# The last stage's second layer as seven block products

## The chip, the cores and the metric

The kernel runs on one core of a Trainium2 chip. The metric is device time in microseconds (us): the time from the start to the end of one execution. The core has five engines with a queue of instructions each, worked off in program order: TensorE (PE in the profile; its weight loads are PEld), VectorE (DVE), ScalarE (ACT), GpSimd (POOL) and SyncE (SP), which here issues the transfers. An engine waits for another only where an instruction needs what the other has yet to write, read or free.

## What is computed

Attention over a window of 64 keys, then a mixture of four experts, then one wide layer with a sloped activation:

```python
x = attention(q, k, v)                         # 1152 tokens x 512
for e in range(4):                             # experts: 512 -> 1024 -> 512
    out += p[:, e:e + 1] * (np.maximum(x @ w1[e], 0) @ w2[e])
x = out
h = x @ w_in                                   # 512 -> 2048
g = np.maximum(h, 0.0) + alpha * np.minimum(h, 0.0)
return g @ w_out                               # 2048 -> 512, alpha: one slope per column of h
```

Inputs are float32 (`w_in` and `w_out` float64, which the kernel converts itself).

## The kernel before, in words

**Precision.** Each float32 operand is kept as two parts that TensorE can multiply: a high part `h` (rounded) and a low part `l` (what rounding left). A product is three matmuls: low x high, high x low, high x high. Making the two parts of a tile is called a split: ACT copies the tile to `h`, and DVE or POOL subtracts `h` from the tile to get `l`.

**Stages.** After the attention, the hidden columns are worked off in 12 stages of 512: stages 0 to 7 are the experts, 8 to 11 the wide layer. `S1` is 8 and `NST` is 12, so the last stage is `s = 11`. The tokens are in two parts, `p = 0` with 512 and `p = 1` with 640. A stage runs through a hand-written list `order`: the first layer for part 0 (units `("A", s, 0, i)`, i from 0 to 6), the first layer for part 1 (`("A", s, 1, i)`), then the second layer for one tile of 128 tokens at a time (`("B", s, p, t)`, four tiles in part 0 and five in part 1).

**First layer.** It is already computed by seven block products instead of eight (`PRODUCTS`, function `product`). Unit i does the product i for both halves of the hidden columns (u = 0, 1), 6 matmuls each, with 256 columns (part 0) or 320 (part 1). The products accumulate in three PSUM banks per u, named X, Z and W; the sequence of banks over i is X, Z, X, W, X, Z, X. After i = 0, 1, 2 ACT copies the bank out (`keep`, L458: tiles s, z, u). After i = 3, 4, 5 DVE adds the bank to the copy (`total`, L462), and the result goes to `evict`; after i = 6 the bank X itself does. So each next use of a bank waits until the copy or the addition before it has read the bank.

**Activation in stages 8 to 11.** `evict` lets ACT make the negative part `r` (L498) and puts the rest in a list. `activate(keep, later)` takes it from there, a few at a time: DVE forms the activated value from `r`, the slope and the source (L541, `heads`), later ACT rounds it to `hh` (L545) and POOL subtracts to get `hl` (L546, `tails`). A part has eight such pieces.

**Second layer.** `l2_unit` makes one token tile by 12 matmuls of 128x512 (four blocks of hidden columns, three matmuls each; L565); DVE adds the bank to `acc` (L588), and in stage 11 SP writes the tile to the output (L590). The very last tile is cut into two halves of 256 columns.

**Order of the work around the matmuls.** Behind each unit's matmuls the program issues: what `settle` holds (the DVE half of earlier weight splits, L215), then the functions that `plan(unit, fn, ...)` hung on that unit, in the order of planning. In stage 11 these are four splits of the second layer's weights: `split_w2`, f = 0 and 1 on the units i = 0 and 1 of part 0, f = 2 and 3 on those of part 1. PSUM has eight banks, handed out in the order in which they were freed.

The functions, with the profile's line numbers:

Of the kernel before, what the change touches and what calls it, by code (L numbers as in the profile page):

```python
# [8 lines left out]
F32 = mybir.dt.float32  # L9
F32R = mybir.dt.float32r  # L10
BF16 = mybir.dt.bfloat16
U32 = mybir.dt.uint32
AF = mybir.ActivationFunctionType
# [13 lines left out]
def tile_kernel(ctx, tc, q, k, v, probs, w1, w2, w_in, w_out, alpha, out):  # L27
# [43 lines left out]
    def psum(name):  # L71
        return pp.tile([P, 512], F32, tag="ps", name=name)
# [419 lines left out]
    def evict(s, p, f, half, src, direct=False):  # L492
        c = slice(half * HALF[p], (half + 1) * HALF[p])
        hh, hl = [x[:, c] for x in h_tiles(s, p, f)]
        if s >= S1:
            col = (s - S1) * NF + f
            r = late["mid"].tile([P, HALF[1]], F32, tag="r", bufs=3, name=f"r{s}_{p}_{f}_{half}")[:, 0:HALF[p]]
            nc.scalar.activation(out=r, in_=src, func=AF.Relu, scale=-1.0)  # L498
            heads.append((hh, hl, r, alph[:, col:col + 1], src, r if direct else src))
            return  # L500
        nc.scalar.activation(out=hh, in_=src, func=AF.Relu)
        lows.append((hl, src, hh))
# [58 lines left out]
    def l2_products(s, p, t, cols, ps):  # L561
        n = 0
        for f in (1, 3, 0, 2) if s == S1 else range(NF):
            for a, b in ((0, 1), (0, 0), (1, 0)):
                nc.tensor.matmul(ps, lhsT=h_t[s, p, f][a][:, t * P:(t + 1) * P], rhs=w_t[2, s, f][b][:, cols],  # L565
                                 start=(n == 0), stop=(n == 3 * NF - 1))
                n += 1

    def l2_unit(s, p, t):

        cut = 2 if (s, p, t) == (NST - 1, 1, NTT[1] - 1) else 1
        w = DM // cut
        for x in range(cut):
            ps = psum(f"o{s}_{p}_{t}")[:, 0:w]
            cols = slice(x * w, (x + 1) * w)
            l2_products(s, p, t, cols, ps)
            l2_out(s, p, t, cols, ps)

    def l2_out(s, p, t, cols, ps):
        at = acc[p][:, t, cols]  # L580
# [20 lines left out]
    with tc.manual_schedule():  # L601
# [59 lines left out]
        def A(s, p):  # L661
            return [("A", s, p, i) for i in range(7)]

        def Bt(s, p):
            return [("B", s, p, t) for t in range(NTT[p])]
# [28 lines left out]
            order += A(s, 0) + A(s, 1) + Bt(s, 0) + Bt(s, 1)  # L694
        order += A(S1, 0) + [("B", S1, 0, t) for t in (2, 3, 0, 1)]
        order += A(S1, 1) + [("B", S1, 1, t) for t in (3, 4, 0, 1, 2)]
        for s in range(S1 + 1, NST):
            order += A(s, 0) + A(s, 1) + Bt(s, 0) + Bt(s, 1)
        at = {u: n for n, u in enumerate(order)}


# [5 lines left out]
        for s in range(1, NST):  # L707
            if s == 1:
                lc, b = [[(k, NCH - 1, t) for t in range(3)] for k in ("LC", "BC")]
                for u in range(2):  # L710
                    plan(lc[u], w_sums, (1, s), s, u, nc.gpsimd)
                for u, part, unit in ((0, A11, ("X1",)), (1, A11, b[0]), (0, SA1, b[0]), (1, SA1, b[1]),
                                      (0, A22, b[2]), (1, A22, b[2])):
                    plan(unit, w_split, (1, s), s, u, part)
            else:
                b = [("B", s - 1, x, t) for x in range(2) for t in range(NTT[x])]
                if s == S1 + 1:
                    b = [("B", S1, 1, t) for t in (3, 3, 4, 4, 0, 1)]
                late_sums = s > S1 + 1
                behind = 2 * (s > S1 + 1)  # L720
                plan(b[1] if behind else ("A", s - 1, 1, 0 if s > S1 else 2), w_sums, (1, s), s, 0, nc.gpsimd)
                for n, part in ((0, A11), (0, A22), (1 + behind, SA1)):
                    plan(b[n], w_split, (1, s), s, 0, part)
                plan(b[2 + behind], w_sums, (1, s), s, 1, nc.gpsimd)
                for n, part in ((2, A11), (3, A22), (4 + behind, SA1)):
                    plan(b[n], w_split, (1, s), s, 1, part)
            units = [(0, 0), (0, 1), (1, 0), (1, 1)]
            if s in (1, S1):
                units = [(int(s == 1), i) for i in (0, 0, 1, 1)]
            for f, (p, i) in enumerate(units):  # L730
                plan(("A", s, p, i), split_w2, (2, s), s, f)

        half = {p: [(0, HALF[p] // 2), (HALF[p] // 2, HALF[p] // 2)] for p in range(2)}
        first, second = half[0]
# [64 lines left out]
        for i, unit in enumerate(order):  # L799
# [9 lines left out]
            if op == "A":  # L809
                product(unit[1], unit[2], 0, unit[3])  # L810
                product(unit[1], unit[2], 1, unit[3])
                if unit[3] == 6:
                    low_parts(0)
                    activate(0, 0 if unit[1] == S1 else 4)
            elif op == "LC":
                l1_chunk(*unit[1:])
            elif op == "BC":
                l2_chunk(*unit[1:])
            elif op == "B":
                activate(0, max(0, len(tails) - 2) if unit[2] == 0 else 0)  # L820
                l2_unit(*unit[1:])
                if unit[1] == S1 - 1:
                    pend.append((i + 2, unit[2], unit[3]))
# [57 lines left out]
```

## Time and profile before

| | us |
|---|---|
| median of 3 runs | 615.28 (614.58 to 616.58) |
| profiled execution, whole | 615.4 |
| its span, first to last instruction | 613.2 |
| PE busy in the span | 604.5 (99%) |
| last stage, first layer, part 0 | 562.75 to 572.82 |
| last stage, first layer, part 1 | 572.82 to 585.14 |
| last stage, second layer | 585.14 to 609.97 |

Times in the profile count from the span's start. A matmul is pipelined: its row lasts longer than the distance to the next one's start, and it is this distance that sets the pace. In rows of instructions, "out<-in" are tiles by name, and the shape is partitions x elements.

### The profile page before, as it was taken

The numbers are of one execution on the slowest core, as the hardware profiler recorded it, in microseconds if no ns is written. First come the engines' busy times: TensorE is split into PE (matmuls) and PEld (weight loads), VectorE is DVE, ScalarE is ACT, GpSimd is POOL, SyncE is SP. The second block draws the span as 40 slices with busy tenths as digits, with TensorE's granted clock in tenths as the row PEclk, the third lists the DMA queues.
The fourth block names the chain that finished last, engine by engine and source line by source line (L and its number), as shares of the span: only waits on it lengthen the run. The fifth ranks groups of instructions, "written<-read, shape, count | busy, mean of one in ns | idle before, by whom it ended". The sixth has DMA issues, their size and how long they took to land.

```text
span 613.2 us, 10950 instructions
## 1 busy us (share of the span) xinstructions
PE 604.5 (99%) x4072; PEld 547.9 (89%) x4072; DVE 469.5 (77%) x946; ACT 318.0 (52%) x795; POOL 271.4 (44%) x278
## 2 busy tenths in 40 slices
PE   6999999999999999999999999999999999999997
PEld 5998999889889889989989989989898988988986
DVE  4887497799798798798698698667968989754642
ACT  5976356426427426426515525436777653642630
POOL 4756502075163254265152452522755585661440
PEclk9999999999999999999999999999999999999999
DMA  9951004234334325324234323012302402400012
GB/s 319 328 200 36 1 1 151 80 110 154 110 103 156 91 98 170 107 70 170 105 100 145 117 87 104 17 69 83 125 1 91 168 18 87 131 25 1 2 54 101
DMA packets 31365, 62.60 MB, mean 102 GB/s; under 512 B 2384, under 2 KB 11344, under 8 KB 30288
## 3 DMA queue, kind: packets, MB, share of 16 engines
q1 hardware_dynamic: 30880, 61.38, 29.7%
q8 instruction: 32, 0.52, 0.4%
q10 hardware_dynamic: 432, 0.52, 0.2%
q14 instruction: 21, 0.17, 0.1%
HBM read 51.14 MB, written 10.75 MB: 101 GB/s over the span
## 4 chain that ended last, share of the span: by engine, by line
PE 97%; DMA 1%; DVE 1%; ACT 0%; POOL 0%; ACTq 0%; issue 0%; POOLq 0%
PE o L565 44%; PE X L451 23%; PE Z L451 11%; PE W L451 6%; PE h L520 4%; PE oc L553 4%; PE pt L360 1%; PE pv L377 1%; PE s L322 1%; DMA kt<-in_k_dram 1%; PE x L598 1%; PE pt L307 0%; ACT p L344 0%; DVE ptr L364 0%; POOL p L353 0%; ACTq L125 0%
## 5 line engine op out<-in xcount | busy, mean ns | idle before, releaser
L565 PE MATMUL o<-w2l,hh 128*128 128x512 f32 (+1 forms) x400 | 155.5, 389 | 0.0
L565 PE MATMUL o<-w2h,hl 128*128 128x512 f32 (+1 forms) x400 | 155.3, 388 | 0.0
L565 PE MATMUL o<-w2h,hh 128*128 128x512 f32 (+1 forms) x400 | 154.9, 387 | 0.0
L294 POOL TENSOR_TENSOR ct<-ct 128x512 f32<-128x512 f32 x32 | 44.2, 1382 | 116.5 <-DVE ct L293 53.6
L565 PEld LDWEIGHTS o<-w2h,hl 128*128 128x128 f32 x400 | 75.1, 188 | 16.7 <-POOL hl L546 1.2
L565 PEld LDWEIGHTS o<-w2h,hh 128*128 128x128 f32 x400 | 75.1, 188 | 14.6
L565 PEld LDWEIGHTS o<-w2l,hh 128*128 128x128 f32 x400 | 75.1, 188 | 14.6
L584 DVE SCALAR_TENSOR_TENSOR acc<-o,pn,acc 128x512 f32<-128x512 f32 x63 | 47.1, 747 | 38.8 <-PE o L565 38.5
L190 POOL TENSOR_TENSOR sr<-ws 128x256 f32<-128x256 f32 x44 | 41.3, 938 | 73.7 <-DVE wfl L215 61.4
L215 DVE SCALAR_TENSOR_TENSOR w2l<-ws,w2h 128x512 fp32r<-128x512 f32 x48 | 44.1, 927 | 19.9 <-ACT w2h L222 19.8
L451 PE MATMUL X<-xth,wfl 128*128 128x256 f32 (+1 forms) x264 | 56.8, 296 | 0.0
L451 PE MATMUL X<-xth,wfh 128*128 128x256 f32 (+1 forms) x264 | 56.6, 295 | 0.0
L451 PE MATMUL X<-xtl,wfh 128*128 128x256 f32 (+1 forms) x264 | 56.6, 295 | 0.0
L222 ACT ACTIVATE wfh<-sr 128x1024 fp32r<-128x1024 f32 x22 | 23.2, 1059 | 53.4 <-POOL sr L190 53.4
L295 POOL TENSOR_TENSOR ct<-ct 128x512 f32<-128x512 f32 x32 | 47.2, 1476 | 2.5
L282 ACT ACTIVATE ct<-wd 128x512 f32<-128x512 f32 x32 | 21.4, 668 | 48.0 <-DVE ct L288 48.0
L588 DVE TENSOR_TENSOR acc<-o,acc 128x512 f32<-128x512 f32 (+1 forms) x28 | 18.8, 670 | 32.9 <-PE o L565 32.8
L451 PEld LDWEIGHTS X<-xth,wfh 128*128 128x128 f32 x264 | 42.6, 190 | 0.0
L451 PEld LDWEIGHTS X<-xtl,wfh 128*128 128x128 f32 x264 | 42.6, 190 | 0.0
L451 PEld LDWEIGHTS X<-xth,wfl 128*128 128x128 f32 x264 | 42.6, 190 | 0.0
L546 POOL TENSOR_TENSOR hl<-s,hh 128x256 fp32r<-128x256 f32 (+1 forms) x16 | 13.3, 851 | 61.3 <-ACT hh L545 61.3
L451 PE MATMUL Z<-xth,wfl 128*128 128x320 f32 (+1 forms) x176 | 37.9, 297 | 0.0
(156 smaller groups left out, 1408.5 us busy)
## 6 DMA issues: line engine op xcount, KB each, us to landing
ws<-in_moe_w_dram SPq DMA_DIRECT2D x16, 1024.0 KB, 6.1
wd<-in_moe_w_in_dram SPq DMA_DIRECT2D x16, 512.0 KB, 3.8
cv<-ct SPq DMA_DIRECT2D x32, 256.0 KB, 2.4
wd<-in_moe_w_out_dram SPq DMA_DIRECT2D x16, 512.0 KB, 3.6
ws<-cv SPq DMA_DIRECT2D x8, 1024.0 KB, 5.2
v<-in_v_dram SPq DMA_DIRECT2D x16, 256.0 KB, 5.8
out_dram<-acc SPq DMA_DIRECT2D x8, 256.0 KB, 2.0
q<-in_q_dram SPq DMA_DIRECT2D x4, 384.0 KB, 6.6
```

Source lines behind the costliest of these rows:

```text
L190: e.tensor_tensor(out=t4[:, o], in0=x, in1=y, op=op)
L215: nc.vector.scalar_tensor_tensor(out=lv, in0=src, scalar=1.0, in1=hv.bitcast(F32), op0=ALU.mult, op1=ALU.subtract)
L222: nc.scalar.activation(out=hv, in_=src, func=AF.Copy)
L282: nc.scalar.activation(out=a, in_=top.bitcast(F32), func=AF.Abs, scale=LIFT)
L294: nc.gpsimd.tensor_tensor(out=y, in0=y, in1=e, op=ALU.mult)
L295: nc.gpsimd.tensor_tensor(out=y, in0=r, in1=y, op=ALU.add)
L451: nc.tensor.matmul(ps, lhsT=w[:, d, :], rhs=x[:, d, :], start=(first and m == 0), stop=(m == 5), skip_group_check=True)
L520: nc.tensor.matmul(ps, lhsT=w[:, d * P:(d + 1) * P], rhs=x[:, d, :], start=(m == 0), stop=(m == 3 * KD - 1))
L553: nc.tensor.matmul(ps, lhsT=h_c[c, f][a][:, t * P:(t + 1) * P], rhs=w_t[2, 0, f][b], start=(n == 0), stop=(n == 3 * NF - 1))
L565: nc.tensor.matmul(ps, lhsT=h_t[s, p, f][a][:, t * P:(t + 1) * P], rhs=w_t[2, s, f][b][:, cols], start=(n == 0), stop=(n == 3 * NF - 1))
L584: nc.vector.scalar_tensor_tensor(out=at, in0=ps, scalar=sc, in1=at, op0=ALU.mult, op1=ALU.add)
L588: nc.vector.tensor_tensor(out=at, in0=ps, in1=at, op=ALU.add)
```

## The change

In stage 11 the second layer of eight of the nine token tiles is also computed by seven block products. The 512 hidden columns, the 512 output columns and 512 tokens of a part are each halved (blocks of 256); `block_product(p, n)` does product n of `BLOCKS` for the two tiles x = 0, 1 of 128 tokens, 6 matmuls of 128x256 each, into banks X, W and Z (two of each), and after every product and x DVE adds the bank to the part of `acc` that it belongs to. The bank goes on accumulating: the sequence is X, W, X, Z, X, Z, X. The units are `("M", p, n)`. The fifth tile of part 1 stays a unit `("B", 11, 1, 4)`, no longer cut in two and now between the two parts.

For these products sums of blocks are needed. `form_sums(key, half)` makes four for the weights (key `"t"`) and four for the activations of each part (keys 0 and 1), two DVE subtractions or additions of 128x512 at a time, out of SBUF tiles into SBUF tiles. `form_split(key, n, engine)` splits one: an ACT copy and a POOL subtraction of 128x512. So that the activated values are there unsplit, DVE's L541 now writes them to a tile of their own (`whole`). The `plan` calls hang this work on units of the first layer and of part 0's products. New `raw` tiles take two buffers in turn (`wd`), the rest lies in tiles that have served their use. In an `M` unit at most one of the `tails` that are left is done ahead of its matmuls.

```diff
@@ -496,7 +496,8 @@
             col = (s - S1) * NF + f
             r = late["mid"].tile([P, HALF[1]], F32, tag="r", bufs=3, name=f"r{s}_{p}_{f}_{half}")[:, 0:HALF[p]]
             nc.scalar.activation(out=r, in_=src, func=AF.Relu, scale=-1.0)
-            heads.append((hh, hl, r, alph[:, col:col + 1], src, r if direct else src))
+            g = whole(p)[:, f, c] if s == NST - 1 else r if direct else src
+            heads.append((hh, hl, r, alph[:, col:col + 1], src, g))
             return
         nc.scalar.activation(out=hh, in_=src, func=AF.Relu)
         lows.append((hl, src, hh))
@@ -567,14 +568,103 @@
                 n += 1
 
     def l2_unit(s, p, t):
-
-        cut = 2 if (s, p, t) == (NST - 1, 1, NTT[1] - 1) else 1
-        w = DM // cut
-        for x in range(cut):
-            ps = psum(f"o{s}_{p}_{t}")[:, 0:w]
-            cols = slice(x * w, (x + 1) * w)
-            l2_products(s, p, t, cols, ps)
-            l2_out(s, p, t, cols, ps)
+        ps = psum(f"o{s}_{p}_{t}")
+        l2_products(s, p, t, slice(0, DM), ps)
+        l2_out(s, p, t, slice(0, DM), ps)
+
+    HC = DM // 2
+    forms, banks = {}, {}
+
+    def whole(p):
+        if ("g", p) not in forms:
+            if p == 0:
+                forms["g", p] = sb.tile([P, NF, LEN[0]], F32, tag="ws", bufs=2, name="g0")
+            else:
+                forms["g", p] = moe.tile([P, NF, LEN[1]], F32, tag="xth0", name="g1")
+        return forms["g", p]
+
+    def form_tiles(key):
+        if key == "t":
+            t = sb.tile([P, 3584], F32R, tag="big", name="th")
+            u = late["wfp"].tile([P, 1024], F32R, tag="sr", bufs=1, name="tl3")
+            hi = [t[:, 2 * HC * n:2 * HC * (n + 1)] for n in range(4)]
+            lo = [t[:, 2 * HC * (4 + n):2 * HC * (5 + n)] for n in range(3)] + [u[:, 0:2 * HC]]
+        elif key == 0:
+            t, (u, w) = xt[0][1].rearrange("p a k t -> p (a k t)"), [x.rearrange("p k t -> p (k t)") for x in xa[0]]
+            hi = [t[:, 2 * HC * n:2 * HC * (n + 1)] for n in range(4)]
+            lo = [y[:, 2 * HC * n:2 * HC * (n + 1)] for y in (u, w) for n in range(2)]
+        else:
+            return [[x[:, n, :, 0:HC] for n in range(4)] for x in xt[1]]
+        return [[x.rearrange("p (f m) -> p f m", f=2) for x in y] for y in (hi, lo)]
+
+    def form_sums(key, half):
+        if half == 0:
+            forms[key] = form_tiles(key)
+            forms[key, "raw"] = []
+        raw = forms[key, "raw"]
+        t = late["mid"].tile([P, 1024], F32, tag="wd", bufs=2, name=f"raw{key}_{half}")
+        raw += [t[:, 2 * HC * n:2 * HC * (n + 1)].rearrange("p (f m) -> p f m", f=2) for n in range(2)]
+        if key == "t":
+            w = ws_t[2, NST - 1]
+
+            def b(i, j):
+                return w[:, 2 * i:2 * i + 2, HC * j:HC * (j + 1)]
+
+            todo = (((b(0, 1), b(0, 0), ALU.subtract), (b(1, 1), raw[0], ALU.subtract)),
+                    ((b(1, 1), b(0, 1), ALU.subtract), (b(1, 0), raw[1], ALU.subtract)))[half]
+        else:
+            g = whole(key)
+
+            def a(i, j):
+                return g[:, 2 * j:2 * j + 2, HC * i:HC * (i + 1)]
+
+            todo = (((a(1, 0), a(1, 1), ALU.add), (raw[0], a(0, 0), ALU.subtract)),
+                    ((a(0, 0), a(1, 0), ALU.subtract), (a(0, 1), raw[1], ALU.subtract)))[half]
+        for n, (x, y, op) in enumerate(todo):
+            nc.vector.tensor_tensor(out=raw[2 * half + n], in0=x, in1=y, op=op)
+
+    def form_split(key, n, e):
+        hi, lo = forms[key]
+        src = forms[key, "raw"][n]
+        nc.scalar.activation(out=hi[n], in_=src, func=AF.Copy)
+        e.tensor_tensor(out=lo[n], in0=src, in1=hi[n].bitcast(F32), op=ALU.subtract)
+
+    BLOCKS = [(("a", 0, 0), ("b", 0, 0), "X", 0, 0), (("a", 0, 1), ("b", 1, 0), "W", 0, 0),
+              (("f", 1), ("f", 1), "X", 0, 1), (("f", 0), ("f", 0), "Z", 1, 1), (("f", 2), ("f", 2), "X", 1, 1),
+              (("f", 3), ("b", 1, 1), "Z", 0, 1), (("a", 1, 1), ("f", 3), "X", 1, 0)]
+
+    def block_product(p, n):
+        s = NST - 1
+        left, right, bank, i, j = BLOCKS[n]
+        cols = slice(HC * j, HC * (j + 1))
+        for x in range(2):
+            first = (p, bank, x) not in banks
+            if first:
+                banks[p, bank, x] = psum(f"m{bank}{p}_{x}")[:, 0:HC]
+            ps = banks[p, bank, x]
+            m = 0
+            for f in range(2):
+                for a, b in ((0, 1), (0, 0), (1, 0)):
+                    if left[0] == "a":
+                        o = HC * left[1] + P * x
+                        lhs = h_t[s, p, 2 * left[2] + f][a][:, o:o + P]
+                    else:
+                        lhs = forms[p][a][left[1]][:, f, P * x:P * (x + 1)]
+                    if right[0] == "b":
+                        rhs = w_t[2, s, 2 * right[1] + f][b][:, HC * right[2]:HC * (right[2] + 1)]
+                    else:
+                        rhs = forms["t"][b][right[1]][:, f, :]
+                    nc.tensor.matmul(ps, lhsT=lhs, rhs=rhs, start=(first and m == 0), stop=(m == 5),
+                                     skip_group_check=True)
+                    m += 1
+            t = 2 * i + x
+            at = acc[p][:, t, cols]
+            nc.vector.tensor_tensor(out=at, in0=ps, in1=at, op=ALU.add)
+            r0 = START[p] + t * P
+            if n == 5:
+                nc.sync.dma_start(out=out[r0:r0 + P, :], in_=acc[p][:, t, :])
+            elif n in (4, 6):
+                nc.sync.dma_start(out=out[r0:r0 + P, cols], in_=at)
 
     def l2_out(s, p, t, cols, ps):
         at = acc[p][:, t, cols]
@@ -694,8 +784,11 @@
             order += A(s, 0) + A(s, 1) + Bt(s, 0) + Bt(s, 1)
         order += A(S1, 0) + [("B", S1, 0, t) for t in (2, 3, 0, 1)]
         order += A(S1, 1) + [("B", S1, 1, t) for t in (3, 4, 0, 1, 2)]
-        for s in range(S1 + 1, NST):
+        for s in range(S1 + 1, NST - 1):
             order += A(s, 0) + A(s, 1) + Bt(s, 0) + Bt(s, 1)
+        s = NST - 1
+        order += A(s, 0) + A(s, 1) + [("M", 0, n) for n in range(7)]
+        order += [("B", s, 1, 4)] + [("M", 1, n) for n in range(7)]
         at = {u: n for n, u in enumerate(order)}
 
 
@@ -729,6 +822,15 @@
                 units = [(int(s == 1), i) for i in (0, 0, 1, 1)]
             for f, (p, i) in enumerate(units):
                 plan(("A", s, p, i), split_w2, (2, s), s, f)
+
+        s = NST - 1
+        for key, sums, unit in (("t", (("A", s, 0, 0), ("A", s, 0, 2)), [("A", s, 0, n) for n in (1, 3, 4, 6)]),
+                                (0, (("A", s, 1, 0), ("A", s, 1, 2)), [("A", s, 1, n) for n in (1, 2, 3, 4)]),
+                                (1, (("M", 0, 0), ("M", 0, 2)), [("M", 0, n) for n in (1, 2, 4, 5)])):
+            for n in range(2):
+                plan(sums[n], form_sums, (2, s) if key == "t" else None, key, n)
+            for n in range(4):
+                plan(unit[n], form_split, None, key, n, nc.gpsimd)
 
         half = {p: [(0, HALF[p] // 2), (HALF[p] // 2, HALF[p] // 2)] for p in range(2)}
         first, second = half[0]
@@ -812,6 +914,9 @@
                 if unit[3] == 6:
                     low_parts(0)
                     activate(0, 0 if unit[1] == S1 else 4)
+            elif op == "M":
+                activate(0, max(0, len(tails) - 1))
+                block_product(*unit[1:])
             elif op == "LC":
                 l1_chunk(*unit[1:])
             elif op == "BC":
```

## Rows read from the trace of the kernel before

**Rows 1.** The page, busy time: engine, us, share of the span, instructions.
```profile
PE 604.5 (99%) x4072; PEld 547.9 (89%) x4072; DVE 469.5 (77%) x946; ACT 318.0 (52%) x795; POOL 271.4 (44%) x278
```

**Rows 2.** The chain of waits, stages 10 and 11: start, length, what, instructions.
```profile
538.40 24.51 PE o L565 x108
...
564.34 1.44 PE Z L451 x12
...
585.31 24.66 PE o L565 x120
```

**Rows 3.** Stretches of stage 11: length; PE, PEld, DVE, ACT, POOL busy; clock; DMA.
```profile
562.75:572.82 10.07, 10.07 (x86) 10.07 (x84) 6.38 (x15) 5.72 (x15) 0.00 (x0) 1.00 0.00 1
572.82:585.14 12.32, 12.32 (x86) 12.32 (x85) 8.52 (x17) 9.24 (x26) 6.49 (x8) 1.00 0.01 1
585.14:609.97 24.83, 24.81 (x122) 20.85 (x120) 7.21 (x12) 3.10 (x9) 6.75 (x8) 1.00 0.23 87
```

**Rows 4.** Timeline of PE, stage 11: start, length, instruction.
```profile
576.34 0.46 PE L451 MATMUL X<-xth,wfl 128*128 128x320 f32 x2
...
585.14 0.40 PE L565 MATMUL o<-w2l,hh 128*128 128x512 f32 x1
...
606.92 0.28 PE L565 MATMUL o<-w2l,hh 128*128 128x256 f32 x1
...
609.67 0.28 PE L565 MATMUL o<-w2h,hl 128*128 128x256 f32 x1
```

**Rows 5.** Lines by form, POOL: shapes, count, busy us, mean ns, idle before.
```profile
L421 POOL TENSOR_TENSOR xtl<-tr,xth 128x512 fp32r<-128x512 f32 x4 | 5.1, 1287 | 7.1 <-ACT xth L420 7.1
```

**Rows 6.** Timeline of DVE, stage 11.
```profile
566.81 0.69 DVE L215 SCALAR_TENSOR_TENSOR w2l<-ws,w2h 128x512 fp32r<-128x512 f32 x1 [0.75 <-ACT w2h L222]
567.98 0.42 DVE L462 TENSOR_TENSOR s<-W,s 128x256 f32<-128x256 f32 x1 [0.47 <-PE W L451]
...
569.04 0.48 DVE L541 SCALAR_TENSOR_TENSOR s<-r,alph,s 128x256 f32<-128x256 f32 x1
...
579.25 0.49 DVE L462 TENSOR_TENSOR s<-W,s 128x320 f32<-128x320 f32 x1 [0.24 <-PE W L451]
...
586.18 0.55 DVE L541 SCALAR_TENSOR_TENSOR r<-r,alph,X 128x320 f32<-128x320 f32 x1 [0.21 <-ACT r L498]
```

**Rows 7.** Timeline of POOL, stage 11.
```profile
573.11 1.44 POOL L546 TENSOR_TENSOR hl<-s,hh 128x256 fp32r<-128x256 f32 x2 [16.08 <-ACT hh L545]
...
585.15 1.73 POOL L546 TENSOR_TENSOR hl<-s,hh 128x320 fp32r<-128x320 f32 x2 [5.54 <-ACT hh L545]
```

**Rows 8.** Timelines of POOL and DVE where both are busy, stages 9 and 10.
```profile
474.89 1.29 POOL L295 TENSOR_TENSOR ct<-ct 128x512 f32<-128x512 f32 x1
475.20 1.27 DVE L541 SCALAR_TENSOR_TENSOR s<-r,alph,s 128x256 f32<-128x256 f32 x1
...
484.24 1.23 DVE L288 SCALAR_TENSOR_TENSOR ct<-wd,ct 128x512 uint32<-128x512 uint32 x1
...
486.53 0.88 DVE L462 TENSOR_TENSOR s<-W,s 128x320 f32<-128x320 f32 x2
...
502.92 1.29 POOL L294 TENSOR_TENSOR ct<-ct 128x512 f32<-128x512 f32 x1
503.01 1.75 DVE L215 SCALAR_TENSOR_TENSOR wfl<-ws,wfh 128x512 fp32r<-128x512 f32 x1
504.29 1.62 POOL L295 TENSOR_TENSOR ct<-ct 128x512 f32<-128x512 f32 x1
504.69 1.78 DVE L288 SCALAR_TENSOR_TENSOR ct<-wd,ct 128x512 uint32<-128x512 uint32 x1
```

**Rows 9.** Timeline of ACT, stage 11.
```profile
572.31 0.42 ACT L498 ACTIVATE r<-u 128x256 f32<-128x256 f32 x1 [0.31 <-DVE u L462]
...
574.39 0.43 ACT L458 ACTIVATE s<-X 128x320 f32<-128x320 f32 x1
...
575.64 0.64 ACT L222 ACTIVATE w2h<-ws 128x512 fp32r<-128x512 f32 x1
```

## The prediction

> **What bounds the kernel now.** I read the busy times first: PE works 99% of the span [rows 1]. Then the chain of waits, to see whether another engine ends last anywhere near the change. In stages 10 and 11 it holds PE alone: a unit of the first layer takes 1.44 us (12 matmuls of 256 columns), the second layer of a whole stage 24.5, the last one 24.66 because of its cut tile [rows 2]. So two things can move the time: the number of matmuls at their pace, and whatever makes PE wait where it waits for nothing today. For the second I read the three stretches of stage 11. VectorE is busy 6.4 of 10.1 us and 8.5 of 12.3 in the first layer, GpSimd not at all and then 6.5, and in the second layer both are mostly free [rows 3]. That looks like room; whether it is, the timelines of the two engines must say, because they turn out to hinder one another.
>
> **What is removed from PE.** A matmul of 512 columns takes 24.51/108 = 0.227 us, one of 256 takes 1.44/12 = 0.120 [rows 2]; the cut tile's 24 matmuls give (609.67 - 606.92)/23 = 0.1196 for exactly the second layer's kind, each with a weight load of its own [rows 4]. The narrow one costs 53% of the wide one. A part's four tiles took 48 x 0.227 = 10.9 us; seven products of 2 x 6 matmuls take 84 x 0.12 = 10.1. That is 0.8 per part, not the eighth that the column count promises. The fifth tile, uncut, takes 2.72 for 2.87. In sum PE needs 1.8 us less. There are 48 weight loads more; they stay behind the matmuls, as they do at this same pace and one load per matmul in both places named.
>
> The Trainium skill, in "TensorE: Matmul & The Clock Gate", section "Back-to-back issue gap", gives a narrower fixed cost: N/2.4 ns plus 2.5 for a matmul on its own. By it the two widths would cost 0.216 and 0.109 us and the change would save about 2.4 us, where the rows give 1.8. It names the case with weight loads as a different one, and the rows have them, so the sum goes by the rows.
>
> **What is added.** Twelve sums on VectorE and twelve splits (ACT copy, GpSimd subtraction), all 128x512; behind the products 28 additions of 256 columns and one of 512, for eight of 512 and two of 256; 13 output transfers for 10. The transfers are on SP, with nothing behind them that computes; the last two are again 128 columns x 256 pieces after the last product, so the tail stays as it is. L541's new target costs nothing: it is the same instruction. ACT's copies cost it time only (below).
>
> Prices on their own: consecutive VectorE rows overlap by 0.07 us (the one at 503.01 ends at 504.76, the next starts at 504.69 [rows 8]), so a two-input operation on 512 columns holds VectorE 0.62 (566.81: 0.69), L541 0.41 on 256 columns and 0.48 on 320, L462 0.35 and 0.42 [rows 6]. A new sum is such a two-input operation. GpSimd: a split of 512 1.29 [rows 5], a low part 0.72 on 256 columns, 0.865 on 320 [rows 7].
>
> **How the two hinder each other.** Rows 8 are to be read in pairs. GpSimd starts at 502.92 and ends at 504.21; VectorE's L215, started at 503.01, takes 1.75 instead of 0.69 and ends 0.55 after GpSimd. GpSimd's next, at 504.29, takes 1.62 instead of 1.29; then VectorE's L288 again 1.78. At 475.20 L541 takes 1.27 instead of 0.48, beside GpSimd's 474.89. Beside GpSimd's shorter work it is 1.23 (484.24). Each waits for the other's whole instruction, and they take turns. It hits VectorE's operations with both inputs in SBUF (the splits' low parts, L541, the new sums), not those that read a PSUM bank (L462 stays at 0.42 to 0.49 throughout) [rows 6, 8]. So for this work the two are one resource, and busy times that look like room add up.
>
> The Trainium skill says the same in "SBUF — State Buffer", section "Who interferes with whom": a VectorE instruction with two SBUF inputs and a GpSimd one that reads SBUF exclude each other for the whole instruction. It is the rule that speaks against this change; the trace agrees (1.75 for 0.69). Were the path shared by halves instead, nothing would be lost while the two together stay below their sum, and the result would be the first rival's.
>
> **The tally.** Two sums for the weights stand in VectorE's queue ahead of the first L462 of part 0, right behind the low part at 566.81, so the count starts at 566.81 + 0.62 = 567.4. It ends at the last two sums for part 1, planned on M(0,2). Behind them in VectorE's queue are the additions of product 3, which must have read bank Z before product 5 can use it. Product 5 would start at 585.14 + 5 x 1.44 = 592.3 [rows 2, 4].
>
> VectorE, two SBUF inputs: 10 sums and 2 low parts x 0.62 = 7.4; 12 L541 = 6 x 0.41 + 6 x 0.48 = 5.3; 12.7 us. GpSimd, ahead of or between them: 4 weight splits 5.2, 8 low parts of part 0 5.8, 4 splits for part 0 5.2, 6 low parts of part 1 (those issued up to M(0,1)) 5.2, the first split for part 1 1.3; 22.6 us. That is 24 operations against 23, so strict turns fit. One after the other they take 35.3: the last sum ends at 602.7, the first of the additions 0.35 later, product 5 starts at about 603.1. It is 10.8 us late.
>
> Where PE would feel it, in order: (1) total u (L462) of unit 5, part 0, ends some 3 us late: two sums and three weight splits stand between, 5.1 us, less the 0.5 that VectorE idles ahead of 567.98 today [rows 6] and what L462 covers. ACT's queue holds the ReLU on it, six more pieces and now a copy of 512 columns (0.64) ahead of the copy of s for part 1. That copy starts 2.1 us after the ReLU today, at 574.39 [rows 9], and must be done before bank X is used again at 576.34 [rows 4]; it has about 1.5 us to spare, 0.9 with the added copy: a stall of about 2 us. (2) In part 1, four sums join the two low parts before the first L462, which today just keeps step (579.25 [rows 6]); bank X's last use waits for L462 of unit 4: about 3 us. (3) In part 0's products the banks wait for additions that stand behind late L541s and the four sums: the rest, some 5 to 6.
>
> After product 5 nothing is late: what GpSimd has left (two low parts and three splits, 5.6 us, done by about 608) is due at product 0 of part 1, 2.88 + 2.72 us after 603.1, and later.
>
> Bounds. Nothing in the rows shows turns kept up for 35 us. If VectorE gets ahead, so that part 1's six low parts and split (6.5) come after its sums, the delay is 4.3. If it loses nothing at all, its own 12.7 plus L462, the four last L541 (they read PSUM) and eight additions, 4.6 + 1.8 + 2.8, end at 589.3, 3.0 before product 5: no delay. Upwards, VectorE also waits for ReLUs that ACT makes late; at 0.21 each (the wait ahead of 586.18 [rows 6]) for all sixteen, 3.4, the delay grows to about 14. I take 10.8: on the rows, wherever both had work, they took turns.
>
> **Sum.** The profiled execution took 615.4; 615.4 - 1.8 + 10.8 = 624.4. It is 0.1 above the median of the runs (615.28), so 624.3. The likeliest case's own range is 617.8 (delay 4.3) to 628 (14).
>
> **Rivals.** A measurement of this kernel can tell about 0.3% (1.85 us) from no change.
> First, on the other side: the lateness is absorbed. VectorE may lose 3.0 us to GpSimd before product 5 waits, and the change breaks even at 4.8 and is measurably slower from 6.6 on, of a possible 13. For it: in stage 9 two L462 stand back to back (486.53 [rows 8]), late, and the chain of waits shows no gap there. Against it: four pairs in rows 8 lose 0.5 to 1.1 each, and 24 operations are exposed. Time 615.4 - 1.8 - 0.1 = 613.5; chance 0.14.
> Second: only stall (1) comes about; once PE is 2 us late, everything behind has that much more room. 615.4 - 1.8 + 2 - 0.1 = 615.5; chance 0.12.
> Third: absorbed, and matmuls of 256 at the page's gap, which would mean a pace of 0.109 where the same loop shows 0.1196 [rows 4]. 615.3 - 2.4 = 612.9; chance 0.04.
> Fourth: GpSimd falls so far behind that part 1's products wait for its low parts and splits too: all its 28.2 and VectorE's 12.7 end at 608.3, with further gaps past 611, where product 2 of part 1 stands: over 628; chance 0.08.
> The change does replace the matmuls; that it would not is no case.
>
> **How the numbers follow.** The forecast has 0.62. Slower by over 0.3%: 0.62 + 0.08 = 0.70. Faster by over 0.3%: the third and a quarter of the first, which lies at -0.29%, 0.04 + 0.04 = 0.08. Same: 0.22. The range takes in the first two rivals, 613.4 to 628, and leaves out the third, the fourth and a little of the forecast's own upper side.
>
> **What would show it.** Right: 256-column matmuls in the second layer at 0.12; VectorE's sums at 1.2 to 1.9 instead of 0.69 and L541 often above 1; PE idle ahead of bank X in part 1's first layer, released by ACT's copy and by L462, and ahead of X and Z in part 0's products, released by additions; part 1's products without a gap. Wrong: sums near 0.69 while GpSimd works (they don't exclude each other there); a chain of PE pieces without gaps (absorbed); or gaps that wait for GpSimd's low parts.

## The result, and the profile after

The changed kernel takes 622.67 us in the median of 4 runs (622.4 to 623.06), beside 614.93 for the kernel before (4 runs): a ratio of 1.0121, 95% interval 1.0101 to 1.0142. It is slower, as forecast, and 1.6 us below the forecast of 624.3. The profiled execution took 622.95 with a span of 621.2. Lines have moved: the products are L657, their additions L662, the sums L624, the new splits L629 (ACT) and L630 (GpSimd); L541, L545, L546 and L565 are now L542, L546, L547 and L566. Stage 11 starts 0.25 later here than before (563.00), which is no part of the change: in the profiled executions of x1 to x4 below, whose work ahead of stage 11 is the same, it starts between 561.87 and 562.98.

The profile page's busy times are to be held against [rows 1]. PE's share fell from 99% to 97%: the span grew by 8 us, PE's busy time by only 1.1.

```profile
PE 605.6 (97%) x4132; PEld 550.7 (89%) x4132; DVE 491.3 (79%) x977; ACT 324.7 (52%) x807; POOL 291.0 (47%) x290
```

Stretches of stage 11, in the columns of [rows 3]: first layer of part 0, of part 1, products of part 0, the rest.

```profile
563.00:573.31 10.31, 10.31 (x86) 10.13 (x85) 8.77 (x14) 6.18 (x15) 2.69 (x2) 1.00 0.00 1
573.31:590.43 17.12, 13.46 (x87) 12.36 (x85) 15.99 (x22) 11.41 (x30) 15.06 (x13) 1.00 0.00 1
590.43:605.17 14.74, 12.02 (x87) 11.66 (x85) 13.48 (x25) 7.04 (x17) 12.86 (x12) 0.88 0.03 10
605.17:618.60 13.43, 12.97 (x98) 12.25 (x96) 7.07 (x16) 0.00 (x0) 1.90 (x2) 1.00 0.39 142
```

Part 1's first layer took 17.12 us instead of 12.32, and VectorE and GpSimd were busy for 93% and 88% of it. Part 0's products took 14.74 where 84 matmuls at 0.12 need 10.1. In the last stretch PE loses nothing.

PE's timeline names each wait in brackets:

```profile
578.62 0.56 PE L451 MATMUL X<-xth,wfl 128*128 128x320 f32 x2 [1.62 <-ACT s L458]
...
582.71 0.56 PE L451 MATMUL X<-xth,wfl 128*128 128x320 f32 x2 [0.24 <-ACT u L458]
...
587.95 0.56 PE L451 MATMUL X<-xth,wfl 128*128 128x320 f32 x2 [1.46 <-DVE z L462]
...
590.43 0.28 PE L657 MATMUL mX<-w2l,hh 128*128 128x256 f32 x1
...
595.60 0.58 PE L657 MATMUL mX<-th,xtl 128*128 128x256 f32 x2 [2.13 <-DVE acc L662]
...
602.23 0.36 PE L657 MATMUL mZ<-w2l,xtl 128*128 128x256 f32 x1 [0.59 <-DVE acc L662]
...
617.86 0.28 PE L657 MATMUL mX<-th,hl 128*128 128x256 f32 x1
```

These are the three kinds of stall of the prediction, in its order. Bank X waits for ACT's copy of s (and for 0.24 us at 582.71 for its copy of u), then for L462 of unit 4 (`z`), and then the products' banks wait for additions. VectorE's timeline shows why they are late:

```profile
567.67 1.79 DVE L624 TENSOR_TENSOR rawt<-ws 128x512 f32<-128x512 f32 x1
569.39 0.68 DVE L624 TENSOR_TENSOR rawt<-ws,rawt 128x512 f32<-128x512 f32 x1
569.99 0.74 DVE L462 TENSOR_TENSOR s<-W,s 128x256 f32<-128x256 f32 x2
...
572.35 1.18 DVE L542 SCALAR_TENSOR_TENSOR g<-r,alph,z 128x256 f32<-128x256 f32 x1
...
582.94 1.23 DVE L624 TENSOR_TENSOR raw<-g 128x512 f32<-128x512 f32 x1
584.09 1.22 DVE L624 TENSOR_TENSOR raw<-g,raw 128x512 f32<-128x512 f32 x1
585.23 0.88 DVE L462 TENSOR_TENSOR s<-W,s 128x320 f32<-128x320 f32 x2
...
587.82 1.16 DVE L542 SCALAR_TENSOR_TENSOR g<-r,alph,s 128x320 f32<-128x320 f32 x1
...
599.98 1.77 DVE L624 TENSOR_TENSOR raw<-g,raw 128x512 f32<-128x512 f32 x1
601.68 0.74 DVE L662 TENSOR_TENSOR acc<-mZ,acc 128x256 f32<-128x256 f32 x2
```

GpSimd's timeline beside it:

```profile
567.63 1.29 POOL L630 TENSOR_TENSOR th<-rawt,th 128x512 fp32r<-128x512 f32 x1 [10.34 <-ACT th L629]
...
581.28 4.64 POOL L547 TENSOR_TENSOR hl<-g,hh 128x256 fp32r<-128x256 f32 x4
585.87 2.76 POOL L630 TENSOR_TENSOR xah<-raw,xtl 128x512 fp32r<-128x512 f32 x2
...
599.47 1.73 POOL L630 TENSOR_TENSOR xtl<-raw,xth 128x512 fp32r<-128x512 f32 x1
```

The first sum of this list began 0.04 after a GpSimd split and took 1.79; the next, with GpSimd idle, took 0.68. L542 at 587.82, beside two splits, took 1.16; before, with GpSimd idle, the same operation took 0.54 (L541 at 580.54). Two pairs of L462 stand back to back, the sign of lateness that [rows 8] showed at 486.53. The two sums at 582.94 and 584.09, beside four GpSimd low parts, start 1.15 apart. The last sum ends at 601.75, the first addition of product 3 follows at once, and PE resumes with product 5 at 602.23.

The chain of waits, for the same places:

```profile
577.72 0.52 ACT th L629
578.24 0.33 ACT s L458
...
583.01 2.30 DVE raw L624 x2
...
599.27 2.48 DVE raw L624 x2
...
605.33 2.76 PE o L566 x12
```

Before, it held PE alone here [rows 2]. Now sums and the new split's ACT copy (`th`, just ahead of s) are links of it.

### The profile page after: what moved, and what is told of

It reads as the page before. It is cut to its first block, busy times and chain, and to the rows that moved or that the text cites. A ratio compares the mean times of both kernels' runs of the same rounds, so it can differ in the third digit from the quotient of the medians.

```text
span 621.2 us, 11142 instructions
## 1 busy us (share of the span) xinstructions
PE 605.6 (97%) x4132; PEld 550.7 (89%) x4132; DVE 491.3 (79%) x977; ACT 324.7 (52%) x807; POOL 291.0 (47%) x290
## 4 chain that ended last, share of the span: by engine, by line
PE 90%; DVE 5%; DMA 2%; ACT 1%; issue 1%; POOL 0%; SPq 0%; ACTq 0%; POOLq 0%
PE o L566 40%; PE X L451 21%; PE Z L451 11%; PE W L451 5%; PE oc L554 4%; PE h L521 4%; DMA kt<-in_k_dram 2%; DVE g L542 1%; PE mX L657 1%; DVE raw L624 1%; PE pv L377 1%; PE s L322 1%; PE pt L360 1%; PE mZ L657 1%; PE x L688 1%; DVE w2l L215 1%
## 5 line engine op out<-in xcount | busy, mean ns | idle before, releaser
L566 PE MATMUL o<-w2l,hh 128*128 128x512 f32 x364 | 142.3, 391 | 0.0
L566 PE MATMUL o<-w2h,hl 128*128 128x512 f32 x364 | 142.2, 391 | 0.0
L566 PE MATMUL o<-w2h,hh 128*128 128x512 f32 x364 | 141.7, 389 | 0.0
L566 PEld LDWEIGHTS o<-w2h,hl 128*128 128x128 f32 x364 | 68.3, 188 | 15.5 <-POOL hl L547 1.2
L566 PEld LDWEIGHTS o<-w2h,hh 128*128 128x128 f32 x364 | 68.4, 188 | 13.6
L566 PEld LDWEIGHTS o<-w2l,hh 128*128 128x128 f32 x364 | 68.4, 188 | 13.4
L215 DVE SCALAR_TENSOR_TENSOR w2l<-ws,w2h 128x512 fp32r<-128x512 f32 x48 | 45.9, 965 | 17.0 <-ACT w2h L222 16.9
L451 PE MATMUL Z<-xth,wfh 128*128 128x320 f32 (+1 forms) x176 | 37.7, 296 | 0.0
L451 PE MATMUL Z<-xtl,wfh 128*128 128x320 f32 (+1 forms) x176 | 37.7, 296 | 0.0
```

The lines of the kernel that those rows point to most:

```text
L215: nc.vector.scalar_tensor_tensor(out=lv, in0=src, scalar=1.0, in1=hv.bitcast(F32), op0=ALU.mult, op1=ALU.subtract)
L451: nc.tensor.matmul(ps, lhsT=w[:, d, :], rhs=x[:, d, :], start=(first and m == 0), stop=(m == 5), skip_group_check=True)
```

## The experiments

The theory: the products save what the rows said, and VectorE's operations with two SBUF inputs and GpSimd's reading ones hold each other up, whole instructions at a time, until PE waits. Rivals: the narrow products are dear in themselves; VectorE's queue is too long with the sums, whatever GpSimd does; GpSimd is busy too long, whatever it does to the memory. All ratios are to the kernel before, measured together with the run: its median was 614.98 beside x1 to x4, 615.03 beside x5, x6, y1 and y2, and 614.78 beside x7 and y4.

**x1: products alone.** The sums and splits are gone; the products read plain blocks.

```diff
-              (("f", 1), ("f", 1), "X", 0, 1), (("f", 0), ("f", 0), "Z", 1, 1), (("f", 2), ("f", 2), "X", 1, 1),
-              (("f", 3), ("b", 1, 1), "Z", 0, 1), (("a", 1, 1), ("f", 3), "X", 1, 0)]
+              (("a", 1, 0), ("b", 0, 1), "X", 0, 1), (("a", 0, 0), ("b", 0, 0), "Z", 1, 1), (("a", 1, 0), ("b", 1, 0), "X", 1, 1),
+              (("a", 1, 1), ("b", 1, 1), "Z", 0, 1), (("a", 1, 1), ("b", 1, 1), "X", 1, 0)]
...
-            for n in range(2):
-                plan(sums[n], form_sums, (2, s) if key == "t" else None, key, n)
-            for n in range(4):
-                plan(unit[n], form_split, None, key, n, nc.gpsimd)
+            pass
```

> Leaves out all sums and splits for the block products; the products that would use them take plain blocks of the same size instead, so matmuls, banks, additions and output transfers are those of the change. Theory (the lateness comes from VectorE and GpSimd shutting each other out while they make the sums and splits; the products themselves are worth 1.8 us): 613 us, no PE gap in stage 11. Rival one (narrow matmuls, or seven products that wait for 28 additions, cost PE the time): 620 or more. Rival two (the split costs of both kinds): between, 615 to 619.

612.25 us, ratio 0.9955 (0.994 to 0.997). Its chain of waits, a product of each part, tile 4 and the end:

```profile
584.82 1.44 PE mX L657 x12
...
594.89 2.75 PE o L566 x12
...
606.27 1.45 PE mX L657 x12
607.75 0.42 DVE acc L662
```

A product is 1.44, so 0.12 per matmul, and PE waits nowhere in the stage. The last matmul starts 2.24 earlier than before (607.43 for 609.67). Of this 0.49 is an earlier start of the stage (562.26 for 562.75), which leaves 1.75 against the predicted 1.8. So the products do save time, and narrow matmuls as the cause fall.

**x2: no low parts of the new splits** and **x3: no sums** each take one of the two partners away.

```diff
 x2
-        e.tensor_tensor(out=lo[n], in0=src, in1=hi[n].bitcast(F32), op=ALU.subtract)
...
-                        lhs = forms[p][a][left[1]][:, f, P * x:P * (x + 1)]
+                        lhs = forms[p][0][left[1]][:, f, P * x:P * (x + 1)]
...
-                        rhs = forms["t"][b][right[1]][:, f, :]
+                        rhs = forms["t"][0][right[1]][:, f, :]
 x3
-        for n, (x, y, op) in enumerate(todo):
-            nc.vector.tensor_tensor(out=raw[2 * half + n], in0=x, in1=y, op=op)
+        forms[key, "src"] = [(b if key == "t" else a)(i, j) for i in range(2) for j in range(2)]
...
-        src = forms[key, "raw"][n]
+        src = forms[key, "src"][n]
```

> Leaves out the twelve GpSimd subtractions of the new splits (the products take the high part in place of the low one); the twelve VectorE sums and the twelve ACT copies stay. Theory: GpSimd's work between the sums falls from 22.6 to 11.0 us, VectorE and GpSimd together end the last sum at 567.4 + 12.7 + 11.0 = 591, before product 5 of part 0 is due: 613.5 to 615. Rival (VectorE's queue is simply too long with twelve more operations, or ACT's with twelve copies): 620 or more.

> Leaves out the twelve VectorE sums; the splits (ACT copy, GpSimd subtraction) stay and take plain blocks as their source. Theory: VectorE has 6.5 us of two-input work left, but fourteen such operations are still exposed to GpSimd's 1.29 us ones; local waits of 1 to 2 us, 614 to 616. Rival (GpSimd's 28 us of work is late by itself and the products wait for low parts): 620 or more.

x2: 616.23, ratio 1.0019 (1.0009 to 1.0028). x3: 616.42, ratio 1.002 (1.0009 to 1.003). Both came out above what I expected, x2 by 1.2 and x3 by 0.4. In x2 the activations' own low parts are still on GpSimd, and they hold the sums up too. VectorE in x2, while GpSimd works off eight low parts without a break from 573.11 to 581.04:

```profile
578.61 0.69 DVE L215 SCALAR_TENSOR_TENSOR w2l<-ws,w2h 128x512 fp32r<-128x512 f32 x1 [0.53 <-ACT w2h L222]
579.22 1.23 DVE L624 TENSOR_TENSOR raw<-g 128x512 f32<-128x512 f32 x1
```

Here one engine holds up the other in turn. The low part that GpSimd began at 578.64 took 1.26 where 0.72 is its price, and L215 beside it kept its 0.69; the sum that followed had to wait, and took 1.23. In x3, where no sum is left, the new splits hold up the activation. GpSimd and VectorE there:

```profile
569.35 1.30 POOL L629 TENSOR_TENSOR th<-ws,th 128x512 fp32r<-128x512 f32 x1 [1.57 <-ACT th L628]
569.61 1.32 DVE L542 SCALAR_TENSOR_TENSOR g<-r,alph,z 128x256 f32<-128x256 f32 x1
```

With x1 and the changed kernel this is nearly a table of two by two: with neither 612.25, with the splits alone +4.2, with the sums alone +4.0, with both +10.4. Together they cost 2.3 more than the sum of the two. It is 1.6 when the profiled executions are counted from the stage's first matmul to its last (45.17, 49.85, 48.54 and 54.86). The table is not clean, because the twelve ACT copies stand in x2 and in x3 as well and so are counted twice in that sum.

**x5: GpSimd busy, but reading nothing.** Each of the twelve new subtractions becomes three fills, which take about as long together.

```diff
-        e.tensor_tensor(out=lo[n], in0=src, in1=hi[n].bitcast(F32), op=ALU.subtract)
+        for m in (2, 2, 1):
+            e.memset(lo[n].bitcast(F32)[:, 0:m], 0.0)
```

> Each GpSimd subtraction of the new splits is replaced by three fills of the same low part with zeros (1280 columns in all), meant to keep GpSimd about as long busy, but reading nothing; sums, copies and products stay. Theory (GpSimd and VectorE exclude each other only where both read SBUF): VectorE is as free as without the subtractions, 616 to 617 (there: 616.2). Rival (GpSimd's own lateness holds up low parts and products): 620 or more.

616.35, ratio 1.0019 (1.001 to 1.0028), the time of x2, where that work is absent. Timelines of GpSimd and VectorE, first beside fills, then beside low parts:

```profile
577.39 1.48 POOL L631 MEMSET tl<- 128x512 f32 x3
577.44 0.69 DVE L215 SCALAR_TENSOR_TENSOR w2l<-ws,w2h 128x512 fp32r<-128x512 f32 x1 [0.59 <-ACT w2h L222]
...
578.84 4.17 POOL L547 TENSOR_TENSOR hl<-g,hh 128x256 fp32r<-128x256 f32 x4
580.05 1.22 DVE L624 TENSOR_TENSOR raw<-g 128x512 f32<-128x512 f32 x1
...
582.95 2.90 POOL L631 MEMSET xah<- 128x512 f32 x6
583.35 0.55 DVE L542 SCALAR_TENSOR_TENSOR g<-r,alph,s 128x320 f32<-128x320 f32 x1
```

So GpSimd's fills (about 1.45 us for three, where a subtraction takes 1.29) cost nothing, and what it reads costs 6.3 (622.67 - 616.35). One reserve: a fill doesn't wait for ACT's copy as the subtraction does, so it can come earlier, and the fills of the first three weight splits ran ahead of the stage, from 557.27 to 561.60. The nine others ran inside it. There the two kernels can be compared in one place: four L542 in a row beside fills (583.35 to 586.49) took 0.54 or 0.55 each, and in the changed kernel, beside subtractions, 1.16 to 1.40. "SBUF — State Buffer", section "Who interferes with whom", in the Trainium skill says that a GpSimd instruction that only writes does not contend with a VectorE one that has two SBUF inputs. The trace agrees (0.55 at 583.35).

**x7: nothing in stage 11 read by GpSimd.** As x2, and the sixteen low parts of stage 11's activations become fills. They wait for no data and are done by 564.7, so that GpSimd is idle for the rest of the stage.

```diff
-            nc.gpsimd.tensor_tensor(out=hl, in0=g, in1=hh.bitcast(F32), op=ALU.subtract)
+            if late.get("last"):
+                nc.gpsimd.memset(hl.bitcast(F32), 0.0)
+            else:
+                nc.gpsimd.tensor_tensor(out=hl, in0=g, in1=hh.bitcast(F32), op=ALU.subtract)
...
+                late["last"] = unit[1] == NST - 1
```

> As the run without the new splits' subtractions (616.2), and in stage 11 the sixteen subtractions for the activations' low parts are also replaced, by fills with zeros that read nothing; VectorE's twelve sums, L541s and additions and all of ACT's copies stay. Theory (the 4 us that remained there over the products alone come from VectorE's sums and L541s waiting for those sixteen): 612.3 to 613.5, sums at 0.69 throughout. Rival (VectorE's or ACT's queue is too long by itself): 615.5 or more.

613.13, ratio 0.9973 (0.9964 to 0.9982). VectorE's sums there:

```profile
579.65 0.69 DVE L627 TENSOR_TENSOR raw<-g 128x512 f32<-128x512 f32 x1
...
588.51 0.68 DVE L627 TENSOR_TENSOR raw<-g 128x512 f32<-128x512 f32 x1
```

All twelve sums are in VectorE's queue, none is held up, and the list of PE's waits in the stage is empty. The rival "VectorE's queue is too long by itself" falls: the sums, with the splits' ACT copies, cost at most 0.9 without a reading GpSimd (613.13 - 612.25) and 4.0 with one (x2).

**x4: the new low parts on VectorE.** The complete computation; the twelve subtractions go through the queue of earlier weight splits.

```diff
-        nc.scalar.activation(out=hi[n], in_=src, func=AF.Copy)
-        e.tensor_tensor(out=lo[n], in0=src, in1=hi[n].bitcast(F32), op=ALU.subtract)
+        split(hi[n], lo[n], src)
```

> Complete kernel; the twelve subtractions of the new splits run on VectorE, 0.62 us each, one unit behind the ACT copy, in place of 1.29 us on GpSimd. Theory (the two are one resource for this work): ahead of the last sums GpSimd keeps 11.0 us, VectorE has 12.7 + 5.6; together 567.4 + 29.3 = 596.7, product 5 about 4.8 us late instead of 9.6 as measured: 616 to 619. Rival (the two do not shut each other out enough to matter and VectorE's queue is the bound): VectorE gets longer, 625 to 630.

622.34, ratio 1.0122 (1.0104 to 1.0139): neither expectation, and no better than the change. GpSimd there:

```profile
574.86 8.21 POOL L547 TENSOR_TENSOR hl<-g,hh 128x256 fp32r<-128x256 f32 x8 [17.60 <-ACT hh L546]
591.51 8.88 POOL L547 TENSOR_TENSOR hl<-g,hh 128x320 fp32r<-128x320 f32 x8 [8.44 <-PE mX L656]
```

GpSimd idles 8.4 us between the two, and still VectorE is late: the last sum ends at 600.93. The theory added the two engines' times over the whole stage. That bounds nothing while one of them has no work; there VectorE's own queue counts, which this edit made four operations longer in each stretch. The rival put the whole bound there, and was too high by 2.7 us or more.

**x6 and y1: the weights' sums earlier.** x6 moves the second pair from unit 2 to unit 0, out of the way of part 0's first L462; y1 puts the weights' sums and splits on the last tiles of stage 10 and units 0 and 1.

```diff
 x6
-        for key, sums, unit in (("t", (("A", s, 0, 0), ("A", s, 0, 2)), [("A", s, 0, n) for n in (1, 3, 4, 6)]),
+        for key, sums, unit in (("t", (("A", s, 0, 0), ("A", s, 0, 0)), [("A", s, 0, n) for n in (1, 3, 4, 6)]),
 y1
-        for key, sums, unit in (("t", (("A", s, 0, 0), ("A", s, 0, 2)), [("A", s, 0, n) for n in (1, 3, 4, 6)]),
+        for key, sums, unit in (("t", (("B", s - 1, 1, 3), ("B", s - 1, 1, 3)),
+                                 [("B", s - 1, 1, 3), ("B", s - 1, 1, 4), ("A", s, 0, 0), ("A", s, 0, 1)]),
```

> Complete kernel; only the second half of the weight sums moves, from unit 2 to unit 0 of part 0's first layer, where VectorE sits idle for about 1 us. Theory (place in VectorE's queue decides): the first L462 is again on time at 568.2 instead of 570.0; the wait for ACT's copy of s in part 1 shrinks from 1.8 us by 1 or more; the rest stays, 621 to 622. Rival (the work as such is too much, wherever it stands): 622.7 unchanged.

> Complete kernel; the weights' four sums and four splits move ahead, to the last two token tiles of stage 10 and the first two units of stage 11, where GpSimd is idle for 16 us and VectorE mostly. Theory: part 0's first layer is on time again and the 2.2 us of waits that it led to are gone; part 1 and part 0's products keep theirs: 618.5 to 620.5. Rival (the work there collides with the weights of the first layer instead): 622 or more.

x6: 620.52, ratio 1.0092 (1.0078 to 1.0106), half a microsecond better than expected. y1: 619.28, ratio 1.0067 (1.0054 to 1.0081). PE in x6, at the first stall:

```profile
576.39 0.56 PE L451 MATMUL X<-xth,wfl 128*128 128x320 f32 x2 [0.27 <-ACT s L458]
```

PE waits 0.27 where it waited 1.62 in the changed kernel. The same work at another place takes most of this stall away, and y1 takes 3.4 us off the whole.

**y2: block products for part 1 alone.** Part 0 keeps its tiles; part 1's sums and splits stand on them, the weights' as in y1.

```diff
-            g = whole(p)[:, f, c] if s == NST - 1 else r if direct else src
+            g = whole(p)[:, f, c] if s == NST - 1 and p else r if direct else src
...
-        order += A(s, 0) + A(s, 1) + [("M", 0, n) for n in range(7)]
+        order += A(s, 0) + A(s, 1) + Bt(s, 0)
...
-                                (0, (("A", s, 1, 0), ("A", s, 1, 2)), [("A", s, 1, n) for n in (1, 2, 3, 4)]),
-                                (1, (("M", 0, 0), ("M", 0, 2)), [("M", 0, n) for n in (1, 2, 4, 5)])):
+                                (1, (("B", s, 0, 1), ("B", s, 0, 1)), [("B", s, 0, n) for n in (1, 2, 2, 3)])):
```

> Complete kernel; block products for part 1 alone, the weights' sums and splits early as in the run beside it, part 1's sums and splits during part 0's four ordinary token tiles (10.9 us in which VectorE and GpSimd are mostly free). Theory (the sums and splits cost nothing where the two engines have room, and the products are worth 0.8 us a part): no PE gap, 1.0 to 1.2 us under the kernel before, 613.7 to 614.0. Rival (the sums always cost something): 615 or more.

613.47, ratio 0.9977 (0.9967 to 0.9987): the whole computation, faster than both kernels. Beside the one before it saves 1.6 us, where 1.0 to 1.2 were expected. From the stage's first matmul to its last it is 1.0 (45.93 for 46.92); most of the rest lies outside the profile's span (see the saving, below). PE waits nowhere in the stage. VectorE's sums there:

```profile
590.64 1.23 DVE L624 TENSOR_TENSOR raw<-g 128x512 f32<-128x512 f32 x1
...
593.12 1.79 DVE L624 TENSOR_TENSOR raw<-g,raw 128x512 f32<-128x512 f32 x1
```

Two of the four are held up, by 0.5 and 1.1, but in the stretch of 12 matmuls to a bank, where nothing waits for them.

**y4: both parts, spread.** Part 0's first layer moves ahead of stage 10's last two tiles, part 0's sums and splits are hung on those tiles, part 1's on the end of part 0's products and on tile 4, and the stage's own weight splits go to units 0 and 1 of part 1.

```diff
-        order += A(s, 0) + A(s, 1) + [("M", 0, n) for n in range(7)]
+        order[-2:] = A(s, 0) + order[-2:] + A(s, 1) + [("M", 0, n) for n in range(7)]
...
-            if s in (1, S1):
-                units = [(int(s == 1), i) for i in (0, 0, 1, 1)]
+            if s in (1, S1, NST - 1):
+                units = [(int(s != S1), i) for i in (0, 0, 1, 1)]
...
+        t3, t4 = [("B", s - 1, 1, n) for n in (3, 4)]
+        for key, sums, unit in (("t", (("A", s, 0, 0), ("A", s, 0, 0)), [("A", s, 0, n) for n in (1, 1, 2, 2)]),
+                                (0, (t3, t3), [t3, t4, t4, ("A", s, 1, 0)]),
+                                (1, (("M", 0, 4), ("M", 0, 5)), [("M", 0, 5), ("M", 0, 6), ("B", s, 1, 4), ("B", s, 1, 4)])):
```

> Complete kernel, block products for both parts. Part 0's first layer of stage 11 moves ahead of the last two token tiles of stage 10; the weights' sums stand on its unit 0 and their splits on units 1 and 2, part 0's sums and splits on those two token tiles and the unit after, part 1's sums on products 4 and 5 of part 0 and their splits on products 5 and 6 and the ordinary tile. Theory (only the place of the sums and splits costs): PE waits less than 1 us in all, of the 1.8 for both parts 1 or more stays, 612.5 to 614. Rival (both parts together are too much for VectorE and GpSimd wherever it stands): 615.5 or more.

614.02, ratio 0.999 (0.9981 to 0.9999), at the upper edge of the range expected (614). Its waits of PE still hold 0.8 us on L462 and 0.5 on an addition:

```profile
PE X L451 <- DVE z L462: 0.8, 1, 0.8
...
PE mX L657 <- DVE acc L662: 0.5, 1, 0.5
```

They add to 1.3 of the 1.8 us by which it stands above x1's 612.25; no order that removes them was tried.

## Why the prediction was right

**The saving.** 1.8 us were predicted and 1.75 measured in x1, at the same pace of 0.12. By the other rule that the prediction weighed, a pace of 0.109, it would have been 2.4; no product shows that pace. Two small terms were missed. The tail is 0.2 to 0.3 us shorter (from the last matmul's start to the span's end it is 3.53 before, 3.34 in the changed kernel, 3.27 in x1). And the time outside the span is 0.4 shorter: time less span is 2.1 to 2.2 in every listed execution of the kernel before and 1.7 to 1.9 in every one with block products; no view shows why. Two slips entered no sum: the weight loads are 60 more (4132 for 4072), not 48, and the row at 484.24 in [rows 8] is L288's, not L541's.

**The turns.** They came as named ahead of time, though not everywhere: of the twelve sums five took 1.2 to 1.8, four 0.77 to 1.10 and three 0.68 or 0.69, and of the twelve L542 with two SBUF inputs six took 1.16 to 1.40. L462, which reads a PSUM bank, kept its 0.41 to 0.48 throughout. That an engine waits for another only for what the other has yet to write, read or free, as the introduction has it, is therefore too narrow: the sum at 567.67 had begun, needed nothing of the split at 567.63, and still took 1.79. That reading by GpSimd is the cause is shown by x5 (busy, not reading: as good as absent) and x7 (nothing read: sums at 0.69, no wait).

**The tally.** It gave 35.3 us, from 567.4 to 602.7; the first held-up sum starts at 567.67 and the last sum ends at 601.75, 34.1 later. That it came this close is partly luck, two errors against each other. Turns with both engines full are cheaper than my prices: 1.15 from sum to sum beside 256-column low parts, where 0.62 + 0.72 is 1.34. And they were not kept up throughout: GpSimd idled 6.9 us in between, in five gaps. x4 shows what the tally is not: a law for any order of the work.

**The delay.** Product 5 was to start 10.8 us late; it started at 602.23 instead of 592.34 + 0.25, which is 9.6 late. By kind:

1. ACT's copy of s cost 2.0, where about 2 were predicted, and 0.2 were lost already in part 0's first layer. Total u, which was to be "some 3 us late", ended 3.0 late (575.44 for 572.22 + 0.25).
2. The later uses of bank X in part 1's first layer cost 2.8, where about 3 were predicted.
3. Part 0's products cost 4.6, where 5 to 6 were predicted: two waits of 2.3 and 0.75 (counted from when the next matmul was due), and 1.56 of matmuls at half the clock (last section). No term foresaw these 1.56, but product 5 waits for the last sum at either clock, so they stand largely in place of a longer wait: the two executions with a mean clock of 1.000 have spans only 0.6 to 0.7 shorter.

After product 5 nothing was late, as predicted. PE ends 9.6 - 1.8 + 0.25 = 8.1 later, and 8.2 was measured (617.86 for 609.67). The term mis-sized is the delay, by 1.2 us: turns cheaper than the plain sum of two instructions took off more than the gaps put on. With the 0.2 of the tail and the 0.4 outside the span, and against them the later start of 0.25, this makes up the 1.6 by which the forecast was too high.

**The rivals.** Absorption was refuted by PE's waits, the single stall by the other two kinds of wait, the smaller pace by x1, and GpSimd's further lag by part 1's products, which run without a gap.

**Open.** The profiled executions of x1 and x7 differ by 1.1 us. About 0.6 of it lies ahead of stage 11 (first matmul at 562.26 and 562.87) and 0.5 in part 0's products, which take 10.56 in x7 and 10.08 in x1, by short gaps of PE that the list of waits doesn't name. What causes either was not traced.

## What to carry to other kernels

Room on two engines is not room if the work put there makes each wait for the other: price a VectorE operation with two SBUF inputs beside a GpSimd one that reads SBUF at both durations, and look at who waits behind it in VectorE's queue. The added work cost 10.4 us (622.67 beside x1's 612.25) where banks wait for VectorE within a unit or two. The two thirds of it that y2 keeps, at other places, made PE wait nowhere. So choose the place by what is queued behind, not by how idle the engines look. A sum of two engines' times bounds a stretch only while both have work waiting; otherwise the longer single queue does.

## What the runs showed of the hardware that was not expected

**A halved clock after a wait.** PE stood idle from 593.3 to 595.6 in the profiled execution of the changed kernel. The stretch behind it (same columns as the windows above):

```profile
595.60:599.18 3.58, 3.58 (x18) 3.58 (x19) 3.55 (x7) 2.35 (x6) 3.58 (x4) 0.53 0.00 0
```

The granted clock was 0.53 on average, nearly all of it at the 1.2 GHz level, and matmuls came 0.213 apart instead of 0.12; from 599.3 on it was 1.00 again. The same is seen behind a wait of 1.9 in x3 (clock 0.55 from 590.29 to 594.12), of 2.1 in y1 (0.57 from 591.27 to 595.28) and of 2.4 in x4 (0.50 from 587.38 to 590.47). It is not seen behind a wait of 2.1 in x6, nor behind x4's later one of 2.3. Two of the four executions of the changed kernel had a mean clock of 1.000 and spans 0.6 to 0.7 us shorter than the two at 0.997; in y1, on the other hand, the execution with the lowest clock (0.996) has the shortest span. So a wait of some 2 us can halve the clock behind it. What decides it, and what it costs in the end, stays open.

**A turn costs less than its two instructions.** It takes 1.15 us per pair where the prices alone add to 1.34, beside a GpSimd at work without a break. y4 shows the same with larger operations: four L215 beside four GpSimd splits start 1.70 apart from the second on (576.66, 578.37, 580.07), where 0.62 + 1.29 is 1.91.
